# A second block product of layer two's token mixing taken as seven smaller ones, from sixteen more kept sums

## The chip, the cores and the metric

The kernel runs on one core of one Trainium2 chip. The metric is the time of one execution on the device, in microseconds (us); the median of several executions counts. The core has five engines with a queue of instructions each: PE (TensorE, matrix products into eight PSUM banks), DVE (VectorE), ACT (ScalarE), POOL (GpSimd) and SP (SyncE, which here only issues DMAs). Each works through its own queue in order and waits on semaphores for the others.

## The reference

One sequence of 2048 tokens with 512 features goes through a linear attention block, a gated MLP block, and both again, with the same weights ("layer one" and "layer two" are the two passes). The change lies in the second pass of this block:

```python
def _B_ref(x, w_in, w_sp, b_sp, w_out):          # x: 2048 x 512, normalised
    z = _gelu(jnp.einsum("bsd,df->bsf", x, w_in))          # 2 x 896 features
    z1 = z[..., :Fh]
    z2 = _layernorm(z[..., Fh:], axis=-1)
    g = jnp.einsum("ts,bsf->btf", w_sp, z2) + b_sp[None, :, None]   # w_sp: 2048 x 2048
    return jnp.einsum("bsf,fd->bsd", z1 * g, w_out)
```

The product with `w_sp` mixes tokens: every output token is a sum over all 2048 input tokens. All is float32.

## The kernel before

**Split operands.** Every float32 operand is taken as a rounded part h (type float32r, made by ACT) and a remainder l (made by DVE as source minus h). A product is three matmuls, h·h, h·l and l·h, added up in one PSUM bank.

**Stages of a layer.** `P1.run` goes over 16 tiles of 128 tokens and makes the attention's sums. `P2.run` goes over the tiles in steps s = 1 to 18, which I call token steps: attention output, layernorm, then `d_high`/`d_low` (the transposed input, split), `e` (the half of `w_in` that gives z2, matmuls of 448 columns), `f` (the half that gives z1, which is stored to DRAM), `e3`/`e4` (statistics and normalisation of z2). z2 stays in SBUF as `ztile[0]` to `ztile[15]`. `P4.run` then mixes tokens, and its last loop over 16 tiles multiplies by `w_out`.

**Mixing as seven products.** Output tokens and input tokens are halved. With 384 features on each side (`H1`, `H2`), the 2x2 block product is taken as seven products P1 to P7 of sums of blocks instead of eight. The 128 features left over (`H3`) go along in three of them (`WITH3`: P4, P1, P5). P3, P5, P6, P7 need sums of blocks of `w_sp`: POOL makes these in layer one (class `Sums`) and stores them to DRAM; both layers read them. P1, P2 and P4 read `w_sp` itself. `ORDERS` sets their order.

**Steps of the mixing.** `P4.run` has one loop over g. An ordinary product is 8 steps (128 input tokens each): 18 matmuls of 512 columns (two output blocks of 512 tokens, three feature tiles, three parts), 24 where `H3` goes along. In step g the kernel calls `prepare(g + 2, g + 3)` (split of the weights of step g+2 and of the tokens of step g+3), `mm(g)`, `fetch(g + 4)` (the DMA of later weights), then `gates()` and, at a product's end, `evac` (PSUM into the accumulators `unit(n, f)` in SBUF). `gates` handles at most one finished unit a step: it loads its z1 on SP, and one step later POOL multiplies (line 1389); a unit that P7 finishes needs a POOL subtraction before (line 1387, `both`).

**The nested product.** One product, P2 (output rows 1024 to 2047, input tokens 1024 to 2047, 512 columns `H1` and `H3`), is itself taken as seven, in 14 steps named "N" with 12 matmuls each (`NEST` gives their order). Three of the seven read `w_sp`; for the other four, sums of quarter blocks are made in layer one by class `Inner`: in 16 units (`todo`), each one DVE addition or subtraction of 128x512, one ACT high part, one DVE low part, two stores. They are read back already split, 1 MB a step, by a DMA that POOL issues (line 1177), so these steps have no weight split. On the token side, `token_sums` and `nested_low` make the sums of tokens, on DVE. Six "quad" buffers hold the weights, 22 "pages" of 128x512 nearly everything else; both are handed out in the order in which they were freed.

**Order around the change.** In layer one, `Inner`'s units stand in the token steps s = 13 to 18 and in the mixing; the nested product comes last, and no gate is handled in its steps 49 to 56. In layer two the order is P4, N, P1, P6, P7, P5, P3:

```python
ORDERS = ("P4", "P1", "P6", "P7", "P5", "P3", "P2"), ("P4", "P2", "P1", "P6", "P7", "P5", "P3")
```

Layer two's token steps also have products of their own (`self.seven`): `side`, `block_sums` and `block_parts`, from s = 14 on. All instructions stand in the order in which the Python code makes them; nothing is reordered by a scheduler.

Of the kernel before, what the change touches and what calls it, by code (L numbers as in the profile page):

```python
# [15 lines left out]
P = 128  # L16
# [40 lines left out]
def mixer_kernel(ctx: ExitStack, tc: tile.TileContext, x_in, wqkv, wo_d, win1_d, win2_d, wsp_d, bsp_d, wout_d,  # L57
# [550 lines left out]
    class P2:  # L608
# [309 lines left out]
        def run(self, sums):  # L918
            w1 = self.win1
            for s in range(1, NT + 3):  # L920
# [28 lines left out]
                else:  # L949
# [37 lines left out]
                if self.seven:  # L987
                    self.side(s)
                elif s == 12:
                    inner.begin(2)  # L990
                elif s == 13 or 15 <= s:
                    inner.unit()
# [61 lines left out]
    class Inner:  # L1054
# [3 lines left out]
        def __init__(self):  # L1058
            self.d = {m: dram.tile([2, P, 2, 2, 512], F32, name=f"n{m}") for m in range(1, 5)}
# [13 lines left out]
        def fetch(self):  # L1073

            if self.ahead:
                k, u = self.ahead.popleft()
                at = (((3, 8), (3, 12)), ((2, 8),), (), ((2, 12),))[u]
                for name, (n, s) in zip(("21", "22") if u == 0 else ("11",) if u == 1 else ("12",), at):
                    self.raw[name] = load(wsp_d[n, s + k])
# [58 lines left out]
    class P4:  # L1138
# [4 lines left out]
        ORDERS = ("P4", "P1", "P6", "P7", "P5", "P3", "P2"), ("P4", "P2", "P1", "P6", "P7", "P5", "P3")  # L1143
# [4 lines left out]
        OWN = {"P1": (2, 8), "P2": (2, 12), "P4": (3, 12)}  # L1148
        SUM = {"P3": 4, "P5": 1, "P6": 2, "P7": 3}

        def __init__(self, p2, sums):
# [5 lines left out]
            for p in self.ORDERS[p2.L]:  # L1157
                if p == "P2":
                    self.steps += [("N", d) for d in range(14)]
                else:  # L1160
                    self.steps += [(p, k) for k in range(HT)]
# [6 lines left out]
            self.wsteps = (48, 50, 51, 53, 55, 56, 57) if self.nest_late else range(54, 61)  # L1168
            self.wloads = (45, 47, 48, 50, 52, 53, 54) if self.nest_late else range(54, 61)

        def fetch(self, g):
# [3 lines left out]
            if p == "N" and self.NEST[k // 2] in self.SUM:  # L1175
                self.w[g] = quads.get([P, 2, 2, 512], F32R)
                nc.gpsimd.dma_start(self.w[g], inner.d[self.SUM[self.NEST[k // 2]]][k % 2])
                return
            t = quads.get([P, 2, 512])
            if p == "N":  # L1180
                n, s = self.OWN[self.NEST[k // 2]]
                s += 2 * (k % 2)
# [32 lines left out]
        def prepare(self, gw, gz):  # L1215
# [4 lines left out]
            if gw is not None:  # L1220
                r = self.raw.pop(gw)
                w = self.w[gw] = quads.get([P, 2, 2, 512], F32R)
                wh, wl = (w[:, :, i] if self.steps[gw][0] == "N" else w[:, i] for i in range(2))
                nc.scalar.activation(wh, r, AF.Copy)  # L1224
            inside = gz is not None and self.steps[gz][0] == "N"
# [25 lines left out]
        def token_sums(self, k):  # L1251
# [3 lines left out]
            a, b = ztile[8 + k], ztile[12 + k]  # L1255
# [3 lines left out]
        def nested_operand(self, g):  # L1259
            name, q = self.NEST[self.steps[g][1] // 2], self.steps[g][1] % 2  # L1260
# [4 lines left out]
            i, c = {"P1": (8, 0), "P2": (12, 0), "P3": (12, 256)}[name]  # L1265
            return name, q, [ztile[i + 2 * q + o][:, c:c + 256] for o in range(2)]
# [10 lines left out]
        def nested_low(self, g):  # L1277
# [7 lines left out]
            for o in range(2):  # L1285
                a, b = ztile[8 + 2 * q + o], ztile[12 + 2 * q + o]
# [7 lines left out]
        def nested_mm(self, g):  # L1294
            name, q = self.NEST[self.steps[g][1] // 2], self.steps[g][1] % 2
# [45 lines left out]
            if name == "P4" and self.nest_late:  # L1341
                self.ready.extend((n, f, False) for n in (2, 3) for f in range(4))

        def mm(self, g):
            p, k = self.steps[g]
            if p == "N":
# [4 lines left out]
            first, last = k == 0, k == HT - 1  # L1351
            if p in self.WITH3 and first:
                self.delta = [banks.get(PAGE) for _ in range(2)]
                self.beta = [[banks.get(PAGE) for _ in range(3)] for _ in range(2)]
# [3 lines left out]
            for j in range(2):  # L1358
                for f in range(3):
                    self.acc(self.beta[j][f], h, l, slice(f * P, (f + 1) * P), w, j,  # L1360
                             first and p in self.WITH3, last)
# [35 lines left out]
        def evac(self, p):  # L1397
# [3 lines left out]
            if p in ("P4", "P1", "P5"):  # L1401
                for j in range(2):
                    n = 2 + j if p == "P1" else j
                    held = p == "P5" or p == "P1" and not self.nest_late
# [4 lines left out]
            for j in range(2):  # L1409
                a, b = 2 + j, j  # L1410
                for f in range(3):
                    q = self.beta[j][f]
                    if p == "P1":
                        V.tensor_add(self.unit(a, f), bs[a] if self.nest_late else self.unit(a, f), q)
                        if not self.nest_late:
                            gates.append((a, f))
                    elif p == "P6":
                        V.tensor_add(self.unit(a, 4 + f), q, bs[a])
                    elif p == "P7":
                        V.tensor_sub(self.unit(b, 4 + f), bs[b], q)  # L1420
# [11 lines left out]
            self.ready.extend((n, f, p == "P7") for n, f in gates)  # L1432

# [53 lines left out]
        def run(self, nxt):  # L1487
# [14 lines left out]
            sums_at = self.steps.index(("N", 0)) - 3  # L1502
            for g in range(n):
# [8 lines left out]
                if self.nest_late:  # L1512
                    self.sums.tick(g, MIX_TICKS)
                    if g == MIX_UNITS[0] - 2:
                        inner.begin(2, 0)
                    if g + 2 in MIX_UNITS:
                        inner.fetch()
                    if g == 34:
                        inner.free = deque(range(8))
                    if g in MIX_UNITS:  # L1520
                        inner.unit(True)
                    elif MIX_UNITS[0] < g < 48:
                        inner.finish(True)
                if g == 3:
                    self.loadb()
                if sums_at <= g < sums_at + 4:
                    self.token_sums(g - sums_at)
# [14 lines left out]
                elif p != "N" and k == HT - 1:  # L1542
                    self.evac(p)
                if self.nest_late and g in (48, 60):
# [38 lines left out]
    inner = Inner()  # L1583
# [44 lines left out]
```

## Time and profile before

| | us |
|---|---|
| median of 3 runs | 1378.05 (1377.92 to 1378.29) |
| profiled execution | 1378.29 |
| its span, first to last instruction | 1376.6 |
| PE busy | 1370.5 |
| DVE busy | 962.5 |
| ACT busy | 606.2 |
| POOL busy | 447.5 |

Busy is time in which an instruction of the engine is under way. PE's matmuls overlap: each is shown with some 0.39 us, while they start about 0.23 us apart, so the starts tell PE's pace and the busy share cannot pass 100%. A DVE or POOL instruction that has begun and is held up counts as busy, too. In a timeline row the first number is the start, the second the length in us; brackets give the idle time of the engine before it and what ended that. A row of windows gives, for a stretch of the span, its length and each engine's busy time in it with the number of instructions.

### The profile page before, as it was taken

The page shows a single profiled execution, that of the slowest core. Times are in us where ns is not written, and L with a number is a line of the kernel's source. Part 1 is how long each engine was busy: PE and PEld are TensorE (multiplying, and loading weights), DVE is VectorE, ACT ScalarE, POOL GpSimd, SP SyncE. Part 2 cuts the span into 40 slices and gives each one's busy share as a digit, 9 for nine tenths or more (in the row PEclk, how much of TensorE's full clock was granted, in tenths as well). Part 3 has the DMA queues.
Part 4 walks back from the last instruction along what each step waited for, and adds up shares of the span by engine and source line. Part 5 has one row for each costly group of instructions (what it writes and reads, how often), then busy time and mean ns, then how long its engine had stood idle before and what let it go on. Part 6 is the DMA issues. An engine that isn't in the chain of part 4 may idle for free.

```text
span 1376.6 us, 17960 instructions
## 1 busy us (share of the span) xinstructions
PE 1370.5 (100%) x6185; PEld 1149.1 (83%) x6185; DVE 962.5 (70%) x1415; ACT 606.2 (44%) x954; POOL 447.5 (33%) x529
## 2 busy tenths in 40 slices
PE   9999999999999999999999999999999999999998
PEld 7888888888888888888888888888888888888887
DVE  6775888665756789887667858876667565775642
ACT  6675544444442442441357655443454342342410
POOL 3343375433233137424123425532220101133310
PEclk9999999999999999999999999999999999999999
DMA  5542377878778988887845414545365744444442
GB/s 173 173 131 62 115 243 254 246 255 279 252 258 285 312 272 275 269 332 249 294 130 152 137 48 143 182 161 164 116 204 178 290 128 135 166 135 155 168 146 91
DMA packets 161435, 267.07 MB, mean 194 GB/s; under 512 B 13760, under 2 KB 57664, under 8 KB 159296
## 3 DMA queue, kind: packets, MB, share of 16 engines
q1 hardware_dynamic: 155440, 242.73, 54.7%
q0 software_dynamic: 4032, 19.92, 4.0%
q10 hardware_dynamic: 1872, 3.28, 0.6%
q8 instruction: 48, 0.79, 0.2%
q14 instruction: 43, 0.35, 0.1%
HBM read 185.40 MB, written 80.48 MB: 193 GB/s over the span
## 4 chain that ended last, share of the span: by engine, by line
PE 99%; DVE 0%; DMA 0%; issue 0%; ACT 0%; DVEq 0%; ACTq 0%
PE bank L120 19%; PE bank L119 19%; PE bank L118 19%; PE bank L1369 11%; PE bank L1367 11%; PE bank L1368 11%; PE bank L1309 2%; PE bank L1311 2%; PE bank L1312 2%; PE bank L832 1%; PE bank L833 1%; PE bank L831 1%; PE bank L256 1%; PE bank L444 0%; DMA qd<-in_wsp_dram 0%; PE bank L475 0%
## 5 line engine op out<-in xcount | busy, mean ns | idle before, releaser
L1367 PE MATMUL bank<-qd,pg 128*128 128x512 f32 x672 | 261.4, 389 | 0.0
L1368 PE MATMUL bank<-qd,pg 128*128 128x512 f32 x672 | 261.4, 389 | 0.0
L1369 PE MATMUL bank<-qd,pg 128*128 128x512 f32 x672 | 261.4, 389 | 0.0
L1234 DVE TENSOR_TENSOR qd<-qd,qd 128x1024 fp32r<-128x1024 f32 x108 | 155.6, 1440 | 103.0 <-ACT qd L1224 101.3
L1224 ACT ACTIVATE qd<-qd 128x1024 fp32r<-128x1024 f32 x108 | 114.3, 1059 | 173.0 <-DMA qd<-s 68.0
L1389 POOL TENSOR_TENSOR bg<-bg,pg 128x512 f32<-128x512 f32 x56 | 83.8, 1504 | 203.3 <-DMA pg<-z 116.6
L120 PE MATMUL bank<-qd,pg 128*128 128x512 f32 x380 | 148.4, 390 | 0.0
L1368 PEld LDWEIGHTS bank<-qd,pg 128*128 128x128 f32 x672 | 126.1, 188 | 26.4
L1369 PEld LDWEIGHTS bank<-qd,pg 128*128 128x128 f32 x672 | 126.1, 188 | 26.1
L1367 PEld LDWEIGHTS bank<-qd,pg 128*128 128x128 f32 x672 | 126.1, 188 | 26.0
L233 POOL TENSOR_SCALAR rs<-mv 128x1 f32<-128x1 f32 x95 | 40.6, 427 | 317.6 <-DVE mv L231 316.1
L1033 POOL TENSOR_TENSOR pg<-pg,pg 128x512 f32<-128x512 f32 x64 | 93.6, 1462 | 138.9 <-DMA pg<-in_wsp_dram 79.6
L104 ACT ACTIVATE pg<-pg 128x512 fp32r<-128x512 f32 (+1 forms) x117 | 72.0, 618 | 130.6 <-DVE pg L295 45.4
L244 ACT ACTIVATE pg<-pg,nb,rs 128x512 f32<-128x512 f32 x63 | 51.1, 810 | 148.8 <-POOL nb L238 138.1
L118 PE MATMUL bank<-qd,pg 128*128 128x512 f32 x284 | 110.7, 390 | 0.0
L119 PE MATMUL bank<-qd,pg 128*128 128x512 f32 x284 | 110.6, 389 | 0.0
L107 DVE TENSOR_TENSOR pg<-pg,pg 128x512 fp32r<-128x512 f32 (+1 forms) x115 | 88.1, 768 | 18.1 <-ACT pg L104 11.2
L118 PE MATMUL bank<-bg,qd 128*128 128x448 f32 x256 | 94.0, 367 | 0.0
L119 PE MATMUL bank<-bg,qd 128*128 128x448 f32 x256 | 93.6, 366 | 0.0
L120 PE MATMUL bank<-bg,qd 128*128 128x448 f32 x256 | 93.4, 365 | 0.0
L295 DVE STREAM_TRANSPOSE pg<-pg 128x512 f32<-128x512 f32 x79 | 85.3, 1080 | 8.2 <-DMA x<-pg 2.3
L118 PE MATMUL bank<-wo,qd 128*128 128x512 f32 x224 | 87.1, 389 | 0.0
(192 smaller groups left out, 2953.4 us busy)
## 6 DMA issues: line engine op xcount, KB each, us to landing
qd<-s SPq DMA_DIRECT2D x64, 512.0 KB, 3.8
qd<-in_wsp_dram SPq DMA_DIRECT2D x44, 512.0 KB, 4.2
pg<-in_wsp_dram SPq DMA_DIRECT2D x80, 256.0 KB, 4.9
s<-pg SPq DMA_DIRECT2D x64, 256.0 KB, 4.4
qd<-n POOLq DMA_DIRECT2D x16, 1024.0 KB, 8.1
pg<-x SPq DMA_DIRECT2D x64, 256.0 KB, 3.5
pg<-z SPq DMA_DIRECT2D x56, 256.0 KB, 4.1
x<-pg SPq DMA_DIRECT2D x48, 256.0 KB, 3.0
```

The lines of the kernel that those rows point to most:

```text
L107: nc.vector.tensor_sub(l, src, h.bitcast(F32))
L118: nc.tensor.matmul(out, ah, bh, start=start, stop=False)
L119: nc.tensor.matmul(out, ah, bl, start=False, stop=False)
L120: nc.tensor.matmul(out, al, bh, start=False, stop=stop)
L295: nc.vector.transpose(y.rearrange("p c (t m) -> p m c t", m=4), r.rearrange("p (m c j) -> p m c j", m=4, c=4))
L1033: nc.gpsimd.tensor_tensor(t, a, b, op=OP.add)
L1224: nc.scalar.activation(wh, r, AF.Copy)
L1234: nc.vector.tensor_sub(wl, r, wh.bitcast(F32))
L1367: m(out, h[:, o], w[:, 0, j, :], start=start, stop=False, skip_group_check=True)
L1368: m(out, h[:, o], w[:, 1, j, :], start=False, stop=False, skip_group_check=True)
L1369: m(out, l[:, o], w[:, 0, j, :], start=False, stop=stop, skip_group_check=True)
L1389: nc.gpsimd.tensor_tensor(u, u, z1, op=OP.mult)
```

## The change

In layer two P1 (output rows 1024 to 2047, input tokens 0 to 1023, 512 columns) is taken as seven, too. There are now two `Inner` objects, `inner["N1"]` for P1 (base 0) and `inner["N2"]` for P2 (base 8), where base is the first of the eight tiles of input tokens. Layer one still computes P1 as before, and nests P2 alone.

- Layer two's order becomes P4, N1, P6, P7, N2, P5, P3: 68 steps instead of 62. N2, which stood second, now follows P7.
- The sixteen units of `inner["N1"]` are made in layer two's token steps 6 to 17: one a step between `d_high` and `d_low`, and one more after `side` in the steps 8, 10, 12, 14 and 16. The 17th call only finishes the 16th unit.
- P1's result no longer stays in PSUM for P6 to add to: N1 writes it to the units, P6 starts its banks anew, and `evac` of P6 adds the unit. `from_first`, called in the first six steps of P7, makes what P7 needs from it (eight DVE instructions of 128x512).

Lines in the order of the file (`onto` is true for N2 alone):

```diff
+            own = inner["N1" if self.seven else "N2"]
...
                         self.d_high(s - 2)
-                        if not self.seven and 14 <= s < 18:
-                            inner.unit()
+                        if 6 <= s < 18 if self.seven else 14 <= s < 18:
+                            own.unit()
                         self.d_low(s - 2)
...
                 if self.seven:
                     self.side(s)
+                    if s == 5:
+                        own.begin(4)
+                    elif s in (8, 10, 12, 14, 16):
+                        own.unit()
...
-        ORDERS = ("P4", "P1", "P6", "P7", "P5", "P3", "P2"), ("P4", "P2", "P1", "P6", "P7", "P5", "P3")
+        ORDERS = ("P4", "P1", "P6", "P7", "P5", "P3", "N2"), ("P4", "N1", "P6", "P7", "N2", "P5", "P3")
...
-                nc.gpsimd.dma_start(self.w[g], inner.d[self.SUM[self.NEST[k // 2]]][k % 2])
+                nc.gpsimd.dma_start(self.w[g], inner[p].d[self.SUM[self.NEST[k // 2]]][k % 2])
...
-                bs = {n: u[n] if self.nest_late else self.bs[2 + (n > 2)] for n in u}
+                bs = {n: u[n] if onto else self.bs[2 + (n > 2)] for n in u}
...
-            if name == "P4" and self.nest_late:
+            if name == "P4" and onto:
                 self.ready.extend((n, f, False) for n in (2, 3) for f in range(4))
...
+            start = first and (p in self.WITH3 or p == "P6" and self.L == 1)
...
                     elif p == "P6":
-                        V.tensor_add(self.unit(a, 4 + f), q, bs[a])
+                        V.tensor_add(self.unit(a, 4 + f), q, bs[a] if self.L == 0 else self.unit(a, f))
                     elif p == "P7":
-                        V.tensor_sub(self.unit(b, 4 + f), bs[b], q)
+                        V.tensor_sub(self.unit(b, 4 + f), bs[b] if self.L == 0 else self.unit(b, 4 + f), q)
                         gates.append((b, f))
...
+        def from_first(self, k):
+            V, (j, f) = nc.vector, divmod(k, 3)
+            if f == 0:
+                V.tensor_add(self.bs[j], self.bs[j], self.bs[2 + j])
+            V.tensor_sub(self.unit(j, 4 + f), self.bs[j], self.unit(2 + j, f))
...
-            sums_at = self.steps.index(("N", 0)) - 3
+            sums_at = [(m, self.steps.index((m, 0)) - 3) for m in ("N1", "N2") if (m, 0) in self.steps]
...
+                if not self.nest_late and p == "P7" and k < 6:
+                    self.from_first(k)
...
-    inner = Inner()
+    inner = {p: Inner(b) for p, b in (("N1", 0), ("N2", 8))}
```

More of the change, by code (lines that the diff above doesn't have):

```diff
@@ L1157, in __init__ @@
             for p in self.ORDERS[p2.L]:
[L1158 to L1161, printed above, removed]
+                self.steps += [(p, k) for k in range(14 if p[0] == "N" else HT)]
             self.T1, self.T2 = {}, {}
@@ L1222, in prepare @@
                 w = self.w[gw] = quads.get([P, 2, 2, 512], F32R)
-                wh, wl = (w[:, :, i] if self.steps[gw][0] == "N" else w[:, i] for i in range(2))
+                wh, wl = (w[:, :, i] if self.steps[gw][0][0] == "N" else w[:, i] for i in range(2))
                 nc.scalar.activation(wh, r, AF.Copy)
-            inside = gz is not None and self.steps[gz][0] == "N"
+            inside = gz is not None and self.steps[gz][0][0] == "N"
             if inside:
@@ L1360, in mm @@
                     self.acc(self.beta[j][f], h, l, slice(f * P, (f + 1) * P), w, j,
-                             first and p in self.WITH3, last)
+                             start, last)
             pages.put(h, l)
```

66 lines of the change are left out of this document (35 added, 31 removed).

## The prediction

> **What bounds the kernel now.** I read the page first: the engines' busy time, the chain that ended last, the costliest group.
>
> ```profile
> span 1376.6 us, 17960 instructions
> PE 1370.5 (100%) x6185; PEld 1149.1 (83%) x6185; DVE 962.5 (70%) x1415; ACT 606.2 (44%) x954; POOL 447.5 (33%) x529
> ...
> PE 99%; DVE 0%; DMA 0%; issue 0%; ACT 0%; DVEq 0%; ACTq 0%
> ...
> L1367 PE MATMUL bank<-qd,pg 128*128 128x512 f32 x672 | 261.4, 389 | 0.0
> ```
>
> The chain is PE for 99% of the span and PE idles nowhere that matters, so the time is the number of matmuls times PE's pace. The 389 ns of a matmul is not its price, because they overlap. Starts give the pace; these two timeline rows are the first matmuls of the nested product's first two steps, 12 matmuls apart:
>
> ```profile
> 1073.74 0.39 PE L1309 MATMUL bank<-qd,pg 128*128 128x512 f32 x1
> ...
> 1076.46 0.39 PE L1309 MATMUL bank<-qd,pg 128*128 128x512 f32 x1
> ```
>
> 2.72 us / 12 = 0.2267 us. Next I cut layer two's mixing at the starts of its products (windows, in this order: N, P1, P6, P7, P5):
>
> ```profile
> 1073.74:1111.83 38.09, 38.09 (x170) 31.55 (x169) 27.75 (x46) 15.70 (x26) 4.24 (x8) 1.00 0.82 299
> 1111.83:1155.34 43.51, 43.51 (x193) 36.05 (x192) 19.56 (x25) 12.86 (x18) 0.00 (x0) 1.00 0.32 101
> 1155.34:1187.98 32.64, 32.64 (x145) 27.04 (x144) 23.28 (x26) 11.37 (x15) 10.35 (x7) 1.00 0.58 194
> 1187.98:1220.62 32.64, 32.64 (x145) 27.04 (x144) 22.45 (x31) 13.40 (x20) 2.58 (x2) 1.00 0.40 129
> 1220.62:1264.14 43.52, 43.52 (x193) 36.05 (x192) 32.19 (x30) 14.09 (x21) 18.90 (x11) 1.00 0.40 133
> ```
>
> The columns are length, then PE, PEld, DVE, ACT, POOL, clock, DMA share, GB/s. N takes 168 x 0.2267 = 38.09 us and P1 192 x 0.2267 = 43.5: both run at PE's pace with the clock granted in full. POOL does nothing in N but issue eight DMAs, and DVE is busy for 73% of it. POOL is busy in P5: those are P7's gates.
>
> **The saving.** P1's 192 matmuls become N1's 168. 24 x 0.2267 = **5.44 us** less on the path. Nothing else on PE changes: P6 starts its banks with a flag instead of a matmul. All below asks what gives part of it back.
>
> **N1 and P6.** N1 stands where N stood, behind P4, with the same work on every engine and the same DMAs, so the first window is its cover: 0. P6 behind it needs less than P1 did: 0. `evac` of P6 is 6 DVE instructions as before. `from_first` adds eight DVE instructions of 128x512 to P7 and the four `token_sums` calls eight of 128x256, about 8 x 0.68 + 8 x 0.42 = 8.8 us by the last two of these groups (the first is ACT's high part, needed below):
>
> ```profile
> L104 ACT ACTIVATE pg<-pg 128x512 fp32r<-128x512 f32 (+1 forms) x117 | 72.0, 618 | 130.6 <-DVE pg L295 45.4
> ...
> L107 DVE TENSOR_TENSOR pg<-pg,pg 128x512 fp32r<-128x512 f32 x8 | 5.5, 684 | 0.0
> L1256 DVE TENSOR_TENSOR pg<-z_z 128x256 f32<-128x256 f32 x4 | 1.7, 419 | 0.0
> ```
>
> P7 then has 22.45 + 8.8 = 31.3 us of DVE work in 32.64, split weights are due two steps (8.2 us) later, and POOL is idle there once P1's gates are gone. Price 0; its cover is 1.3 us, and if that failed DVE would enter N2 late by as much.
>
> **The units in the token steps.** Each of the 16 adds one DVE sum and one DVE low part (2 x 0.68 = 1.37 us), one ACT part (0.62 us), one 256 KB load on average and two 256 KB stores on SP's queue. The stretches between successive `e` groups (from s = 6; s = 8; s = 16; s = 17; then two of layer one, where the same units already run):
>
> ```profile
> 867.33:880.38 13.05, 13.05 (x61) 11.27 (x60) 11.31 (x20) 5.66 (x10) 7.24 (x12) 1.00 0.69 214
> 893.44:906.49 13.05, 13.05 (x61) 11.27 (x60) 8.87 (x16) 4.94 (x8) 3.74 (x8) 1.00 0.50 161
> 985.62:993.24 7.62, 7.62 (x38) 6.76 (x36) 5.59 (x12) 4.45 (x7) 1.93 (x6) 1.00 0.32 107
> 993.24:1002.21 8.97, 8.97 (x43) 7.89 (x42) 7.48 (x15) 3.64 (x6) 3.09 (x8) 1.00 0.52 145
> 282.29:295.34 13.05, 13.05 (x62) 11.26 (x60) 8.52 (x15) 6.05 (x11) 3.19 (x6) 1.00 0.84 287
> 308.39:318.73 10.34, 10.34 (x50) 9.02 (x49) 7.36 (x14) 4.86 (x8) 3.91 (x8) 1.00 1.00 356
> ```
>
> With one or two units a stretch DVE has 11.31 + 0.7, 8.87 + 2.7, 5.59 + 2.7 and 7.48 + 0.7 us: over only at s = 16 (8.3 in 7.62), and s = 18 lies behind it. ACT has room everywhere (4.45 + 1.2 of 7.62 at s = 16). The tightest place is there, the transpose and low part that the `e` at 993.24 waits for:
>
> ```profile
> 987.44 1.07 DVE L295 STREAM_TRANSPOSE pg<-pg 128x512 f32<-128x512 f32 x1
> 990.33 0.69 DVE L107 TENSOR_TENSOR qd<-pg,qd 128x512 fp32r<-128x512 f32 x1 [1.82 <-ACT qd L104]
> ...
> 993.64 0.36 PE L120 MATMUL bank<-bg,qd 128*128 128x448 f32 x1
> ```
>
> The low part is ready at 991.02, 2.62 us before the first matmul that reads it. The unit stands between the two DVE rows, so its 1.37 us fall into the 1.82 us in which DVE waits for ACT. What the units of s = 14 and 15 leave over goes into the 2.62. DMA rises by 48 x 256 KB, about 90 GB/s over s = 6 to 17; layer one's stretches run at 287 and 356 GB/s with PE full. Price 0. Upper end: three units before that low part with nothing hidden, 4.1 - 2.62 = 1.5.
>
> **P7 into N2: what is late next.** P7's six gates used to fall into P5, steps of 5.44 us; now they fall into N2's steps of 2.72 us. SP is no obstacle, since N2's four middle products are fetched by POOL, so the z1 loads run ahead. But POOL's two instructions a gate meet DVE's splits. In P5 the timeline shows how they do (DVE rows, POOL rows, then POOL's two groups):
>
> ```profile
> 1217.42 4.09 DVE L1420 TENSOR_TENSOR bg<-pg,bank 128x512 f32<-128x512 f32 x6 [2.38 <-PE bank L1369]
> ...
> 1225.43 1.79 DVE L1240 TENSOR_TENSOR pg<-pg,pg 128x512 fp32r<-128x512 f32 x1
> 1227.14 1.64 DVE L1212 TENSOR_TENSOR pg<-z_z,z_z 128x384 f32<-128x384 f32 x1
> ...
> 1230.44 0.55 DVE L1212 TENSOR_TENSOR pg<-z_z,z_z 128x384 f32<-128x384 f32 x1
> ```
>
> ```profile
> 1218.19 1.29 POOL L1387 TENSOR_TENSOR bg<-bg 128x512 f32<-128x512 f32 x1 [28.52 <-DVE bg L1420]
> 1225.25 1.42 POOL L1389 TENSOR_TENSOR bg<-bg,pg 128x512 f32<-128x512 f32 x1 [5.76 <-DMA pg<-z]
> 1226.62 1.74 POOL L1387 TENSOR_TENSOR bg<-bg 128x512 f32<-128x512 f32 x1
> ```
>
> ```profile
> L1389 POOL TENSOR_TENSOR bg<-bg,pg 128x512 f32<-128x512 f32 x23 | 33.6, 1466 | 130.6 <-DVE qd L1234 68.8 <-DMA pg<-z 54.9 <-DVE bg L1428 4.3
> L1387 POOL TENSOR_TENSOR bg<-bg 128x512 f32<-128x512 f32 x6 | 12.1, 2023 | 28.5 <-DVE bg L1420 28.5
> ```
>
> They take turns. L1212 takes 0.55 us alone and 1.64 beside POOL; it ends 1.56 us after the L1240 before it (1227.22 to 1228.78), so POOL's turn cost DVE 1.56 - 0.55 = 1.01 us. The evacuation from PSUM at 1217.42 keeps 0.68 each with POOL at work.
>
> Let T be N2's start. Step d starts at T + 2.72 d and needs its low part 0.45 us later. POOL issues two DMAs first, the second when step 0 frees a buffer, 3.18 us in as in these rows of N, and 0.53 long; its first gate starts at T + 3.7:
>
> ```profile
> 1074.20 0.54 POOL L1177 DMA_DIRECT2D qd<-n  x1 [58.63 <-PE bank L1369]
> 1076.92 0.53 POOL L1177 DMA_DIRECT2D qd<-n  x1 [2.19 <-DVE qd L1234]
> ...
> DMA to landing us min/median/max: 5.0/7.1/8.4
> ```
>
> From there to the deadline of step 7 (T + 19.5) are 15.8 us. DVE has one weight split, four token splits and six half-width sums to do: 1.2 + 4 x 0.68 + 6 x 0.42 = 6.5 us. POOL's nine or ten turns take 9.1 to 10.1. Together 15.6 to 16.6: **0 to 0.8 us late**. Step 8 (18.5 us; DVE 8.0; POOL ten or eleven turns) comes to 18.1 to 19.1, the same. I take 0.8, because the quoted turns are strict. Lower end 0: POOL's DMA issues leave DVE free turns. Upper end: each turn costs POOL's full 1.30 us, 10 x 1.30 + 6.5 = 19.5, which is 3.7 late.
>
> POOL's own lateness is a second danger in the same place: its DMA for step 11 stands behind all six gates. With turns of 1.01 and some 0.5 us of DVE between, six gates and five DMA issues take 6 x 3.0 + 5 x 0.53 = 20.7 us: it is issued at T + 24.4 and lands 5.0 us later, at 29.4; step 11 starts at 29.9. At the groups' means (6 x 3.49 + 5 x 0.53 = 23.6) it lands 2.4 late, inside the upper end above, because PE held up at step 7 moves this deadline too. On SP the loads of N2's last two steps stand behind the six z1 loads; they are issued by step 8 or so and due at step 12: 0. N2 into P5 is N into P1 with one more 0.55 us sum a step. The single gates of N2 follow in P5, fewer than now: 0.
>
> **Sum.** -5.44 + 0.8 = -4.6 us. The profiled execution (1378.29, of it 1376.6 span) would go to 1373.7; it lies 0.24 above the median, so I forecast 1378.05 - 4.6 = **1373.4 us**. Ends: 1372.6 (nothing given back) and 1378.05 - 5.44 + 3.7 + 1.5 = 1377.8.
>
> **Rivals.**
> 1. *N2's turns cost POOL's whole instruction.* 3.7 us given back: 1376.3, of the size of no change. For it: strict turns, and twelve POOL instructions in six steps. Against: 1.01, not 1.30, in the rows above. The Trainium skill, SBUF — State Buffer, section "Who interferes with whom", says that a DVE instruction with two SBUF inputs and a GpSimd one that reads SBUF exclude each other for the whole instruction; by its rule the time is this rival's. The trace agrees on the exclusion and on PSUM inputs being free of it, and shows a shorter turn.
> 2. *Slower: units block DVE in the token steps.* A unit's sum waits at the head of DVE's queue for its load, and `d_low` stands behind it. Two units in a step leave some 6 us from load to use; loads of this kind take 4.5 us in layer one (row below), on an SP queue that also waits for ACT and DVE. Each step in which DVE is held for 0.65 us beyond the slack (2.6 to 5) costs that; over twelve steps 7.8 us, so 1381.2. It turns into a slowdown beyond 4.6 us. Against: layer one, full PE with the same units.
> 3. *The change doesn't do what it says.* 24 matmuls fewer is certain, so this has no share.
>
> ```profile
> pg<-in_wsp_dram SPq DMA_DIRECT2D x11, 256.0 KB, 4.5
> ```
>
> **How the numbers follow.** Forecast 0.66, with its own range 1372.4 to 1375.0; rival 1 0.22 (1375.0 to 1377.8); rival 2 0.12. A difference within 0.2% (2.76 us) is what a measurement of this kernel can hardly tell from none, so "faster" means below 1375.3: the forecast's share and some of rival 1, 0.70; same 0.18; slower 0.12. The range reaches from the forecast's lower end through most of rival 1: 1372.4 to 1377.2.
>
> **What would show it.** PE loses 24 matmuls and N1 takes 38.1 us. If I am right on N2, DVE's token splits there last 1.4 to 1.8 us, POOL is busy in its steps 1 to 8, and N2 takes 38.1 to 40.4 us with PE gaps only near steps 5 to 8 or 11. Rival 1 shows as N2 near 42 us; rival 2 as stretches between `e` groups longer than 13.05 and 10.33. I am wrong if PE idles in N1, P6, P7 or P5, or if the steps after N2 start late on weight splits.

## The result, and the profile after

The changed kernel takes 1384.49 us (median of 5 runs, 1383.84 to 1385.64) against 1378.05 for the kernel before (5 runs, 1377.92 to 1378.65): a ratio of 1.0047, 95% interval 1.0032 to 1.0062. It is slower by 6.4 us where 4.6 us less were forecast. The page of the changed kernel, its span, engines and chain:

```profile
span 1383.9 us, 18136 instructions
PE 1370.4 (99%) x6161; PEld 1145.6 (83%) x6161; DVE 998.5 (72%) x1487; ACT 617.0 (45%) x980; POOL 460.8 (33%) x537
...
PE 89%; DVE 5%; DMA 2%; ACT 2%; issue 1%; POOL 1%; SPq 0%; ACTq 0%; DVEq 0%; POOLq 0%
```

PE has its 24 matmuls less, but the chain, 99% PE before, now runs for a tenth of the span through other engines: somewhere PE waits. The windows of the changed kernel find the places: first the four stretches from the `e` of s = 14 to that of s = 18, then N1, P6, P7, N2, P5 (columns as in the prediction).

```profile
965.88:975.17 9.29, 9.14 (x43) 7.70 (x41) 6.65 (x12) 3.28 (x7) 2.87 (x6) 1.00 0.68 242
975.17:987.41 12.24, 10.83 (x48) 8.86 (x48) 8.52 (x15) 5.48 (x10) 3.43 (x6) 1.00 0.54 173
987.41:997.41 10.00, 8.15 (x36) 6.61 (x36) 8.23 (x17) 4.97 (x9) 2.90 (x6) 1.00 0.55 184
997.41:1008.42 11.01, 10.95 (x43) 9.21 (x43) 10.73 (x21) 6.62 (x11) 3.24 (x6) 0.85 0.76 234
1080.89:1118.97 38.08, 38.08 (x169) 31.53 (x168) 27.46 (x46) 15.37 (x26) 4.23 (x8) 1.00 0.83 303
1118.97:1151.61 32.64, 32.64 (x145) 27.03 (x144) 18.81 (x26) 11.91 (x17) 0.00 (x0) 1.00 0.41 130
1151.61:1184.25 32.64, 32.64 (x145) 27.03 (x144) 27.41 (x45) 13.56 (x21) 0.00 (x0) 1.00 0.41 138
1184.25:1227.73 43.48, 40.55 (x169) 32.49 (x168) 41.11 (x50) 13.72 (x24) 21.55 (x20) 0.96 0.84 294
1227.73:1271.25 43.52, 43.52 (x193) 36.04 (x192) 28.71 (x31) 15.17 (x23) 11.10 (x8) 1.00 0.44 146
```

The same four stretches took 8.97, 10.33, 7.62 and 8.97 us before (the last two rows stand in the prediction, the first two are these):

```profile
966.32:975.29 8.97, 8.97 (x43) 7.89 (x42) 5.57 (x9) 4.19 (x7) 2.12 (x6) 1.00 0.44 139
975.29:985.62 10.33, 10.33 (x49) 9.01 (x48) 7.59 (x15) 3.45 (x6) 1.25 (x4) 1.00 0.27 79
```

So 6.65 us are lost in the last token steps, a place that the prediction priced at 0. N2 takes 43.48 us instead of 38.09: 5.4 us lost, where 0.8 was expected. N1, P6, P7 and P5 are as forecast. With 0.9 us more at the start of the mixing (at 1040, where PE waits for DVE's late additions), -5.44 + 6.65 + 5.4 + 0.9 = +7.5 us; the span grew by 7.3. This profiled execution is the longest of the five (1385.64 us). In it PE's granted clock fell to half twice for 3.4 us, at 999.2 and 1207.4; the two executions with a mean granted clock of 1.000 took 1383.84 and 1383.90 us, so the slowdown does not rest on that.

**The token steps.** The first rows are from the timelines of the kernel before, tile 15 of the layernorm: the last of POOL's three small instructions (L233, L234, L238), then ACT's normalising (L244). The second group is the same tile after the change, on DVE, POOL, ACT and PE. (The line of an instruction can differ from kernel to kernel, since lines were added.)

```profile
988.66 0.27 POOL L238 TENSOR_SCALAR nb<-mv,rs 128x1 f32<-128x1 f32 x1
...
988.97 0.81 ACT L244 ACTIVATE pg<-pg,nb,rs 128x512 f32<-128x512 f32 x1 [1.37 <-POOL nb L238]
```

```profile
993.73 1.10 DVE L295 STREAM_TRANSPOSE pg<-pg 128x512 f32<-128x512 f32 x1
994.68 0.67 DVE L107 TENSOR_TENSOR pg<-pg,pg 128x512 fp32r<-128x512 f32 x1
995.27 0.66 DVE L1125 TENSOR_TENSOR pg<-pg,pg 128x512 f32<-128x512 f32 x1
997.39 0.69 DVE L107 TENSOR_TENSOR qd<-pg,qd 128x512 fp32r<-128x512 f32 x1 [1.46 <-ACT qd L104]
...
993.97 0.22 POOL L233 TENSOR_SCALAR rs<-mv 128x1 f32<-128x1 f32 x1 [0.93 <-ACT pg L839]
...
994.94 1.05 POOL L238 TENSOR_SCALAR nb<-mv,rs 128x1 f32<-128x1 f32 x1
...
996.03 0.81 ACT L244 ACTIVATE pg<-pg,nb,rs 128x512 f32<-128x512 f32 x1 [2.09 <-POOL nb L238]
996.75 0.61 ACT L104 ACTIVATE qd<-pg 128x512 fp32r<-128x512 f32 x1
...
995.22 0.39 PE L833 MATMUL bank<-qd,bg 128*128 128x512 f32 x1
997.41 0.47 PE L118 MATMUL bank<-bg,qd 128*128 128x448 f32 x1 [1.80 <-ACT qd L104]
```

The unit's low part and sum do start in DVE's gap behind the transpose. But POOL's `nb` is under way at that very time and takes 1.05 us instead of 0.27: it ends at 995.99, 0.06 us after the second of the two. ACT's normalising waits for `nb`, ACT's high part of the transposed input (of the tile before) queues behind it, DVE's low part and PE's `e` wait for that. So the gap does not fill: DVE still waits 1.46 us in it. From the end of DVE's aggregate (L231) to the end of `nb` it took 1.68 us for tiles 5 to 12 and 1.40 for 13 to 15 before; with a unit beside it, 2.74 and 2.17. Every step starts a little later on DVE, the lag adds up (layernorm's addition of tile 13 3.4 us later than before, of tile 15 6.3), and once it has used up the slack PE idles.

**N2.** DVE's, POOL's and PE's timelines around the longest gap, and the windows of that gap and behind it (L1395 and L1397 are a gate's subtraction and multiplication, L1387 and L1389 in the kernel before):

```profile
1200.46 1.77 DVE L107 TENSOR_TENSOR pg<-pg,pg 128x512 fp32r<-128x512 f32 x1
1202.27 3.00 DVE L1295 TENSOR_TENSOR pg<-z_z,z_z 128x256 f32<-128x256 f32 x2
...
1206.39 1.00 DVE L107 TENSOR_TENSOR pg<-pg,pg 128x512 fp32r<-128x512 f32 x1
...
1202.24 1.30 POOL L1395 TENSOR_TENSOR bg<-bg 128x512 f32<-128x512 f32 x1
1203.62 1.36 POOL L1397 TENSOR_TENSOR bg<-bg,pg 128x512 f32<-128x512 f32 x1
...
1204.96 0.39 PE L1317 MATMUL bank<-qd,pg 128*128 128x512 f32 x1
1207.44 0.79 PE L1318 MATMUL bank<-qd,pg 128*128 128x512 f32 x1 [2.09 <-DVE pg L107]
```

```profile
1204.96:1207.44 2.48, 0.39 (x3) 0.00 (x1) 2.45 (x5) 0.63 (x1) 2.38 (x4) 1.00 0.95 295
1207.44:1210.95 3.51, 3.51 (x8) 2.80 (x9) 3.51 (x6) 1.74 (x5) 1.61 (x2) 0.51 1.09 422
```

DVE is held by POOL's turns and its low part of step 7 comes at 1207.39, 23.1 us into N2 instead of 19.5. The gap before it is 2.48 us from start to start; the next eight matmuls then start 0.43 us apart at a granted clock of 0.51. In this execution that adds some 1.6 us to the waits.

### The profile page after: what moved, and what is told of

It reads as the page before. It is cut to its first block, busy times and chain, and to the rows that moved or that the text cites. A ratio compares the mean times of both kernels' runs of the same rounds, so it can differ in the third digit from the quotient of the medians.

```text
span 1383.9 us, 18136 instructions
## 1 busy us (share of the span) xinstructions
PE 1370.4 (99%) x6161; PEld 1145.6 (83%) x6161; DVE 998.5 (72%) x1487; ACT 617.0 (45%) x980; POOL 460.8 (33%) x537
## 4 chain that ended last, share of the span: by engine, by line
PE 89%; DVE 5%; DMA 2%; ACT 2%; issue 1%; POOL 1%; SPq 0%; ACTq 0%; DVEq 0%; POOLq 0%
PE bank L120 17%; PE bank L119 17%; PE bank L118 17%; PE bank L1375 10%; PE bank L1377 10%; PE bank L1376 10%; PE bank L1318 2%; PE bank L1315 2%; PE bank L1317 2%; DVE st L229 1%; DVE pg L107 1%; DMA qd<-in_wsp_dram 1%; PE bank L256 1%; DVE pg L1293 0%; POOL nb L238 0%
## 5 line engine op out<-in xcount | busy, mean ns | idle before, releaser
L1375 PE MATMUL bank<-qd,pg 128*128 128x512 f32 x608 | 236.8, 389 | 0.4 <-DVE pg L893 0.2
L1376 PE MATMUL bank<-qd,pg 128*128 128x512 f32 x608 | 236.6, 389 | 0.0
L1377 PE MATMUL bank<-qd,pg 128*128 128x512 f32 x608 | 236.6, 389 | 0.0
L1238 DVE TENSOR_TENSOR qd<-qd,qd 128x1024 fp32r<-128x1024 f32 x106 | 149.6, 1412 | 89.1 <-ACT qd L1228 88.6
L104 ACT ACTIVATE pg<-pg 128x512 fp32r<-128x512 f32 (+1 forms) x141 | 86.8, 619 | 163.4 <-DVE pg L295 48.3
L120 PE MATMUL bank<-qd,pg 128*128 128x512 f32 x380 | 148.4, 391 | 0.0
L233 POOL TENSOR_SCALAR rs<-mv 128x1 f32<-128x1 f32 x95 | 41.4, 436 | 315.0 <-DVE mv L231 313.5
L1375 PEld LDWEIGHTS bank<-qd,pg 128*128 128x128 f32 x608 | 114.1, 188 | 24.8 <-DVE pg L893 1.2
L1377 PEld LDWEIGHTS bank<-qd,pg 128*128 128x128 f32 x608 | 114.2, 188 | 23.7
L1376 PEld LDWEIGHTS bank<-qd,pg 128*128 128x128 f32 x608 | 114.2, 188 | 23.7
L1397 POOL TENSOR_TENSOR bg<-bg,pg 128x512 f32<-128x512 f32 x56 | 85.4, 1532 | 144.3 <-DMA pg<-z 123.5
L244 ACT ACTIVATE pg<-pg,nb,rs 128x512 f32<-128x512 f32 x63 | 51.0, 810 | 154.9 <-POOL nb L238 149.5
L118 PE MATMUL bank<-qd,pg 128*128 128x512 f32 x284 | 110.7, 390 | 0.0
L119 PE MATMUL bank<-qd,pg 128*128 128x512 f32 x284 | 110.6, 389 | 0.0
L107 DVE TENSOR_TENSOR pg<-pg,pg 128x512 fp32r<-128x512 f32 (+1 forms) x139 | 101.1, 729 | 10.0 <-DMA z<-pg 4.9
```

The costliest lines, as they stand in the source:

```text
L104: nc.scalar.activation(h, src, AF.Copy)
L107: nc.vector.tensor_sub(l, src, h.bitcast(F32))
L118: nc.tensor.matmul(out, ah, bh, start=start, stop=False)
L119: nc.tensor.matmul(out, ah, bl, start=False, stop=False)
L120: nc.tensor.matmul(out, al, bh, start=False, stop=stop)
L1238: nc.vector.tensor_sub(wl, r, wh.bitcast(F32))
```

## The experiments

Two losses, two questions: does each come from where the timelines point (units beside POOL's chain; turns beside DVE in N2), and is that all that stands between the seven products and their gain? Where an expectation gives a theory a letter, its own words say which theory is meant. "Lost" below is by how much PE's starts lie further apart than 0.227 us (512 columns) or 0.205 us (448), summed over a place. The kernel before ran beside each group on the same chip: 1377.82, 1377.82, 1377.80 and 1378.0 us.

**Without the units.** Layer two's calls of `own.unit()` go, and N1 multiplies N2's stored sums in place of its own.

```diff
-                        if 6 <= s < 18 if self.seven else 14 <= s < 18:
+                        if not self.seven and 14 <= s < 18:
                             own.unit()
...
-                    if s == 5:
-                        own.begin(4)
-                    elif s in (8, 10, 12, 14, 16):
-                        own.unit()
...
-                nc.gpsimd.dma_start(self.w[g], inner[p].d[self.SUM[self.NEST[k // 2]]][k % 2])
+                nc.gpsimd.dma_start(self.w[g], inner["N2"].d[self.SUM[self.NEST[k // 2]]][k % 2])
```

> The changed kernel without its sixteen units in layer two's token steps; N1 reads the kept sums that layer one made for the other block, so P1's values are wrong: what is left out is the making of N1's own sums. Theory (two separate losses: the units delay the token steps 14 to 17, and P7's gates delay N2): the four stretches between e groups that grew go back to 8.97, 10.33, 7.62 and 8.97 us, N2 still takes some 43 us; time 1384.5 - 6.7 - 0.9 (the late additions before the mixing) = about 1377. Rival (the units' DMAs or sums also cost later, or N2's loss is a consequence of the token steps): N2 is short too, about 1372.5. Rival (the loss in the token steps has another cause than the units): 1384.

1377.63 us, ratio 1.0000 [0.9991, 1.0009]. The four stretches are 8.97, 10.33, 7.61 and 8.97 us again, and N2 still loses 5.4. The units cost 6.9 us (1384.49 against 1377.63), and N2's loss does not come from the lag that they leave.

**The gates out of N2.** `gates` isn't called in g = 38 to 45, so the turns come later.

```diff
-                if not (self.nest_late and 49 <= g < 57):
+                if not (49 <= g < 57 if self.nest_late else 38 <= g < 46):
                     self.gates()
```

> The changed kernel with no gate handled in N2's steps 38 to 45, as layer one does it in its nested steps; the same work, eight steps later. Theory (POOL's turns against DVE make N2 late): N2 back to 38.1 us, token steps unchanged; 1384.5 - 5.3 = about 1379. Rival (N2 is late because of its weights or P7's evacuation): N2 stays at 43 us, 1384. Rival (the turns only move into P5): P5 grows by as much as N2 shrinks, 1384.

1388.33 us, ratio 1.0077 [1.0063, 1.0090]: worse. The profiled execution is the shortest of the five (1384.79); in it N2 takes 38.08 us, but P5 takes the loss, 6.1 us at its start:

```profile
1182.74:1220.82 38.08, 38.08 (x169) 31.54 (x168) 31.18 (x46) 11.01 (x19) 16.50 (x16) 1.00 0.92 338
1220.82:1270.43 49.61, 45.67 (x193) 36.97 (x192) 36.02 (x36) 17.87 (x27) 19.46 (x13) 0.97 0.37 132
```

The turns only moved, to the last 11 us of N2 and on into P5, where DVE splits the weights of P5's first steps (2.3 us each beside POOL, 1.2 alone) and evacuates N2's last sums behind them. What the longer executions lose in addition is open.

**Both edits.**

> Both edits together (N1's own sums left out as before). Theory: nothing gives the saving back, 1378.05 - 5.4 = 1372.6, at most 0.5 more. If the sum of the two is not met by more than 1 us, the two losses hang together.

1380.52 us, ratio 1.0020 [1.0012, 1.0029], 8 us above the expected 1372.6. The one loss left in layer two is 6.3 us at P5's start (in the profiled execution, 1378.73, the shortest): this run still holds the turns, only later, so it can't show whether the two losses add up. The run without units and with the gates in P5, below, does.

**All units early**, two a step in s = 6 to 13, none in the short last steps.

```diff
-                        if 6 <= s < 18 if self.seven else 14 <= s < 18:
+                        if 6 <= s < 15 if self.seven else 14 <= s < 18:
...
-                    elif s in (8, 10, 12, 14, 16):
+                    elif 6 <= s < 14:
```

> The changed kernel with its units two a step in steps 6 to 13, none in the short steps 15 to 17; same work. Theory A (the units fail because of the short steps, where DVE has no room): the token steps lose nothing, 1384.5 - 7.6 = about 1377. Theory B (each unit delays DVE's part for good and the delay adds up over the steps, so that where they stand hardly matters): the e groups of steps 10 to 14 are late instead, 1384 or more.

1387.08 us, ratio 1.0070 [1.0057, 1.0082]. The delay comes sooner: POOL's chain takes 2.74 us in six of these eight steps, DVE is 9.4 us late at tile 11, and the stretch of s = 12 takes 14.96 us instead of 13.05. Room in DVE's busy time (8.87 of 13.05 us at s = 8) is not what limits.

**Gates in P5.** None in g = 38 to 50, two a step in g = 51 to 59 (P5 is g = 52 to 59). All turns but one (at 1202.40) leave N2; the next is at 1224.82, 1.7 us into P5, when DVE has the splits for P5's first steps behind it.

```diff
-                if not (self.nest_late and 49 <= g < 57):
-                    self.gates()
+                if not (49 <= g < 57 if self.nest_late else 38 <= g < 51):
+                    self.gates(2 if not self.nest_late and 51 <= g < 60 else 1)
```

> The changed kernel with no gate handled in N2 from its first step on and two a step in the first P5 steps; same work. N2 had 27.8 us of DVE work in 38.1 us before, and twelve POOL turns of 1.01 us do not fit beside it; P5's stretch of 43.5 us has room for all fourteen gates (20 turns). Theory: N2 back to 38.1 us, P5 not longer than 44; the units' loss stays, so 1384.5 - 5.3 = about 1379. Rival (DVE is late in P5 instead, as when the gates were put eight steps later): P5 grows by 4 or more, 1383 to 1385.

1380.52 us, ratio 1.0020 [1.0011, 1.0030], 1.5 us above the expected 1379, but N2 and P5 run at PE's pace:

```profile
1185.08:1223.15 38.07, 38.07 (x169) 31.54 (x168) 30.67 (x50) 13.60 (x24) 5.53 (x9) 1.00 0.82 302
1223.15:1266.67 43.52, 43.52 (x193) 36.05 (x192) 42.77 (x31) 15.17 (x23) 34.66 (x19) 1.00 0.50 183
```

The first row also gives DVE's work in N2 with a single turn beside it: 30.67 us. In the changed kernel the same 50 instructions took 41.11, so the eleven further turns cost 10.4 us, 0.95 each, and 30.67 + 10.4 does not fit into 38.08. P5 bears the turns: DVE is busy there for 42.77 of 43.52 us and PE loses nothing.

**Half the turns.** The subtraction ahead of a gate (`both`) is left out in layer two, so that N2 has six POOL instructions instead of twelve.

```diff
-                if both:
+                if both and self.L == 0:
```

> The changed kernel without POOL's subtraction in P7's gates of layer two (left out: one of the two terms of those six units), so six POOL turns in N2 instead of twelve. Theory (turns): DVE's waits there fall from 12.2 us to 6, N2 loses at most 0.5 us, time about 1379.5. Rival (POOL's DMAs for the sums are issued too late): half the work before each issue helps them as well, but then the waits that end last in N2 are on those DMAs and not on DVE.

1383.48 us, ratio 1.0039 [1.0024, 1.0054]. N2 still loses 4.1 us, so the loss does not go with the number of turns; DVE is busy there for 37.80 us, so the five turns more than in the run before cost 7.1 us. DVE's and POOL's timelines:

```profile
1190.59 5.79 DVE L1293 TENSOR_TENSOR pg<-z_z,pg 128x256 f32<-128x256 f32 x2
1196.30 1.28 DVE L1330 TENSOR_TENSOR bg<-bank,bg 128x512 f32<-128x512 f32 x2
...
1190.87 1.30 POOL L1397 TENSOR_TENSOR bg<-bg,pg 128x512 f32<-128x512 f32 x1
1192.10 0.59 POOL L1181 DMA_DIRECT2D qd<-n  x1
1192.72 1.30 POOL L1397 TENSOR_TENSOR bg<-bg,pg 128x512 f32<-128x512 f32 x1
1193.95 0.59 POOL L1181 DMA_DIRECT2D qd<-n  x1
```

Two additions of 0.42 us take 5.79 (the first alone 4.39): it stays out over two of POOL's instructions and the DMA issues behind them, at which DVE gets no turn either. PE then idles: the start after 1194.49 comes 2.6 us later, at 1197.08, 0.1 us after the first of the two evacuations that stand behind the additions (L1330). The trace puts no wait of PE in N2 on a DMA of the sums, as the rival would have it.

**Units without DVE's two instructions** (the low part replaced by a second copy on ACT, the additions and subtractions left out).

```diff
-            low(l, t, h)
+            if self.base:
+                low(l, t, h)
+            else:
+                high(l, t)
...
-                nc.vector.tensor_add(t, self.raw["21"], t)
+                if self.base:
+                    nc.vector.tensor_add(t, self.raw["21"], t)
...
```

> The changed kernel whose units keep their loads, stores and buffers but have no DVE instruction: no sum is made, and the low part is a second copy by ACT (left out: N1's own sums). Theory (DVE's time, with or without POOL's small instructions behind it): the four late e groups of the token steps are on time again, 1384.5 - 7.5 = about 1377. Rival (the 12 MB of DMA or SP's longer queue make the transposed inputs late): they stay late, 1384.

1378.96 us, ratio 1.0009 [1.0000, 1.0018]. The stretches are 8.97, 10.33, 7.61 and 8.97 us and POOL's chain 1.68 and 1.40: loads, stores, SP's queue and ACT's parts are not the cause there. The time stays 1.3 us above the run without units; 0.65 of that shows in the trace at 1020, where PE waits for loads of `win_sums` that POOL issues.

**Units with one-input DVE instructions.** As above, with a statistics instruction (`bn_stats`) over the same 512 columns in place of each DVE instruction; nobody reads its result.

```diff
+        def look(self, t):
+            st = small.tile([P, 1, 6], F32, name="st", tag="st1")
+            nc.vector.bn_stats(st[:, 0, :], t)
...
-            low(l, t, h)
+            if self.base:
+                low(l, t, h)
+            else:
+                high(l, t)
+                self.look(h.bitcast(F32))
...
-                nc.vector.tensor_add(t, self.raw["21"], t)
+                if self.base:
+                    nc.vector.tensor_add(t, self.raw["21"], t)
+                else:
+                    self.look(t)
...
```

> The same, but with a statistics instruction of one SBUF input and the same length (0.69 us for 128x512) in the place of each DVE sum and low part. Theory A (DVE's time alone): the token steps lose as much as in the changed kernel, 6 to 7 us, about 1384. Theory B (the two-input instructions take turns with POOL's three small instructions between statistics and normalisation, which grew from about 1.4 to 2.2 us): the loss falls by 0.7 us a step and more, to 3 us or less, about 1380. Rival (DMA): as in the changed kernel, and also without DVE work.

1380.46 us, ratio 1.0017 [1.0008, 1.0027]. DVE spends the same time in the gap, but POOL is not held, and the low part follows after 0.72 us of waiting (DVE's and POOL's timelines, tile 15):

```profile
990.48 1.22 DVE L1074 BATCH_NORM_STATS2 st<-pg 128x6 f32<-128x512 f32 x2
992.42 0.69 DVE L107 TENSOR_TENSOR qd<-pg,qd 128x512 fp32r<-128x512 f32 x1 [0.72 <-ACT qd L104]
...
990.75 0.27 POOL L238 TENSOR_SCALAR nb<-mv,rs 128x1 f32<-128x1 f32 x1
```

The four stretches are as before. DVE's time as such fits the gap; what does not fit is two-input instructions beside POOL's chain. DVE's lag of 2.1 us at tile 15 remains and costs 2.0 us at 1017, where PE waits for loads of `win_sums`: POOL issues the first of them at 998.3, behind its small instructions, and at 996.2 in the kernel before.

**Units behind the layernorm.** The gates as in the fifth run, and a 128x1 copy of `nb` on DVE ahead of each unit, which makes DVE wait for the end of POOL's chain.

```diff
+            self.last_nb = self.ms[i][2]
...
                         if 6 <= s < 18 if self.seven else 14 <= s < 18:
+                            if self.seven:
+                                see = small.tile([P, 1], F32, name="see")
+                                nc.vector.tensor_copy(see, self.last_nb)
                             own.unit()
```

> With two turns a step of P5 in place of N2's, and in the token steps a 128x1 copy of the layernorm's last result (nb) on DVE ahead of each unit, so that DVE's unit instructions cannot start before POOL's chain has ended. Theory B (the unit's two-input instructions hurt only by holding POOL's layernorm chain): the chain stays at 1.68 and 1.40 us from aggregate to nb, the unit's 1.37 us fall beside ACT's normalising and high part (0.85 + 0.62 = 1.47 us), the four last token stretches come back to 8.97, 10.33, 7.61 and 8.97 us within 0.3 each, and the time is 5.4 us below before less what the later stretches keep: 1372.5 to 1375. Rival (it is DVE's added time in these steps, wherever it stands): the stretches stay as in the run with the turns in P5, and the time stays at 1380 to 1381.

1375.58 us, ratio 0.9984 [0.9975, 0.9992]: 2.2 us faster than the kernel before, 4.9 faster than the run with the gates in P5, 8.9 faster than the changed kernel. The interval excludes 1, so a difference below the 0.2% of the prediction can be told here. DVE's and POOL's timelines of tile 15, then the windows of the stretches of s = 16 and 17:

```profile
991.97 0.15 DVE L973 COPY see<-nb 128x1 f32<-128x1 f32 x1 [0.43 <-POOL nb L238]
992.04 0.68 DVE L107 TENSOR_TENSOR pg<-pg,pg 128x512 fp32r<-128x512 f32 x1
992.64 0.69 DVE L1129 TENSOR_TENSOR pg<-pg,pg 128x512 f32<-128x512 f32 x1
993.34 0.69 DVE L107 TENSOR_TENSOR qd<-pg,qd 128x512 fp32r<-128x512 f32 x1
...
991.67 0.27 POOL L238 TENSOR_SCALAR nb<-mv,rs 128x1 f32<-128x1 f32 x1
```

```profile
985.47:993.36 7.89, 7.78 (x37) 6.57 (x36) 7.28 (x17) 3.95 (x7) 2.12 (x6) 1.00 0.60 204
993.36:1002.85 9.49, 9.43 (x42) 7.92 (x43) 9.31 (x19) 6.79 (x11) 3.33 (x6) 1.00 0.71 231
```

An added wait of 0.43 us makes the step shorter: `nb` takes 0.27 us, the unit runs beside ACT's two instructions, and the low part follows without a gap. The stretches of s = 14 and 15 are back at 8.97 and 10.33 us, those of s = 16 and 17 at 7.89 and 9.49, the last 0.5 too long; so the time lies a little above the expected 1372.5 to 1375. A lag of 3.5 us against the run without units (below) is left at tile 15, and 1.5 us are lost around 1020, where PE waits for the loads of `win_sums`: POOL issues the first at 999.67, in the run without units at 995.74.

**Units behind the low part**, on the gates of the fifth run.

```diff
-                        if 6 <= s < 18 if self.seven else 14 <= s < 18:
+                        if not self.seven and 14 <= s < 18:
                             own.unit()
                         self.d_low(s - 2)
+                        if self.seven and 6 <= s < 18:
+                            own.unit()
```

> With two turns a step of P5 in place of N2's, and the token steps' unit behind DVE's low part of the tile in place of ahead of it. Theory B: POOL's chain of the same tile is over by then and stays at 1.68 and 1.40 us; the gap of 1.82 us ahead of the low part stays unused, and the unit's 1.37 us come on top of DVE's other work of the step. In the steps in which DVE has 1.4 us to spare nothing is lost; the last three stretches may grow by up to 1.4 us each: 1373 to 1378. Rival (added DVE time, wherever it stands): as the run with the turns in P5, 1380 to 1381.

1388.88 us, ratio 1.0081 [1.0067, 1.0095]: neither expectation. POOL's chain is 1.68 and 1.40 us as Theory B has it, and yet this is the slowest of all. The gap stays empty and a second one opens (DVE's and ACT's timelines):

```profile
931.33 0.56 DVE L752 TENSOR_TENSOR z_z<-z_z 128x384 f32<-128x384 f32 x1 [1.77 <-ACT z_z L244]
...
941.61 0.69 DVE L107 TENSOR_TENSOR qd<-pg,qd 128x512 fp32r<-128x512 f32 x1 [1.51 <-ACT qd L104]
...
942.82 0.68 DVE L1131 TENSOR_TENSOR pg<-pg,pg 128x512 f32<-128x512 f32 x1
...
943.54 0.63 ACT L104 ACTIVATE pg<-pg 128x512 fp32r<-128x512 f32 x1 [1.96 <-DVE pg L1131]
944.08 1.12 ACT L244 ACTIVATE z_z<-z_z,nb,rs 128x896 f32<-128x896 f32 x1
```

ACT's high part of the unit now comes late, z2's normalising queues behind it on ACT, and DVE's next step waits for that (the row at 931.33, of the step before: 1.77 us, where the run with the gates in P5 waits 0.85). Holding POOL's chain is the cause in the changed kernel, but not the only way to lose: a step is a loop through DVE, POOL, ACT and DVE again, and what is put on the loop can lengthen it.

**No units, gates in P5** (edits of the first and fifth runs; N1 reads N2's sums).

> With two turns a step of P5 in place of N2's, and no second set of sums made (N1 multiplies N2's sums, so the output's half is not the reference's): what the seven products are worth when neither loss is there. If the two losses are all that stood against the saved 5.44 us: 1372.4 to 1373.0. If a third stands behind them (N1's own loads or evacuations, P5's added turns): above 1374.

1372.97 us, ratio 0.9964 [0.9951, 0.9976], PE on 98% of the chain. The two losses were all that stood against the saving, up to 0.6 us (1377.80 - 5.44 = 1372.4). That the forecast 1373.4 lies near is luck: it has 0.8 us for turns in N2, of which this run has one.

**Second units in the long steps**, in s = 7, 8, 10, 11, 12 in place of 8, 10, 12, 14, 16, on the kernel with the copy of `nb`.

> The run with the units behind the layernorm, with the five second units of a step moved from the steps 8, 10, 12, 14 and 16 to 7, 8, 10, 11 and 12, so that none stands in the short last steps (10.33 and 7.61 us). Theory (what is left there, 0.7 us at 993, 1.54 at 1018 and 0.53 at 1036, is DVE's own lag, 3.5 us at tile 15, from too much work in the last short steps): the lag at tile 15 falls under 2 us, one to two microseconds come back: 1373.3 to 1374.7. Rival (the lag is bound to the number of units, and comes from the earlier steps as well): the lag is only moved ahead, and the time is that of the run before, 1375 to 1377.

1375.81 us, ratio 0.9985 [0.9976, 0.9994], no gain. DVE's lag against the run without units is 4.4 us at tile 12 (2.0 without this edit) and 4.6 at tile 15 (3.5): the rival held, the lag is only moved ahead. The 2.6 us between the run with the copy and the one without units are the price of the sixteen units, at their best place among those tried.

## Why the prediction missed

- **The saving, N1, P6 and P7, P5: right.** 24 matmuls less, N1 in 38.08 us, P6 and P7 in 32.64 each with `from_first` in P7, P5 in 43.52.
- **The units: wrong, and the largest error.** The step that failed is the one that lets the units' 1.37 us of a step fall into the gap in which DVE waits for ACT and prices them at 0. The gap was there because a chain ran through POOL, and the units' instructions lengthen that chain: 1.68 to 2.74 and 1.40 to 2.17 us. I had used the rule that a two-input DVE instruction and a POOL instruction exclude each other, but only for POOL's large gates; POOL's instructions of one column, a few tenths of a microsecond each, I overlooked. The Trainium skill, SBUF — State Buffer, section "Who interferes with whom", states the exclusion without a lower limit of size; the trace agrees (`nb` 0.27 to 1.05 us), and so do the run with one-input instructions and the one with the units behind `nb`.
- **Counting DVE's busy time per stretch was the wrong test.** "11.31 + 0.7" or "8.87 + 2.7" in 13.05 says nothing where DVE's step is a loop with waits in it. The second and third rows of the changed kernel's windows show it: DVE busy for 8.52 of 12.24 and 8.23 of 10.00 us, and PE late; so do the runs with the units early and behind the low part.
- **Rival 2's size was right and its mechanism wrong.** It priced the token steps at 7.8 us; 6.65 and 0.9 came, which is luck. Only the first unit waited for its load (0.86 us at 872.85, with PE on time): without DVE's two instructions the same loads and stores cost nothing in these steps and 1.3 us in all.
- **N2: mechanism right, size wrong.** POOL's turns, DVE's late low part of step 7 and a PE gap there are as described. The mis-sized term is DVE's 6.5 us up to step 7: it leaves out the four evacuations from PSUM that stand between (0.64 us each, 2.55 in all). From POOL's first gate to the end of step 7's low part DVE took 19.4 us where 15.8 were to be had. 8.7 of them are its own work, evacuations included, so POOL's eleven turns cost 0.97 us each on average, as I had it (1.01, with nine or ten); the low part came 3.6 us late, the size of rival 1 by luck, which had ten turns of 1.30 and no evacuations. The lower end assumed that POOL's DMA issues leave DVE free turns; the run with half the turns shows a DVE addition that got none at two of them. The whole of N2 would have shown it sooner: N's 27.75 us of DVE and twelve turns of 1.01 make 39.9, over 38.09. And the restart at half clock, 1.6 us in the profiled execution, was not foreseen.
- **The rivals were taken one at a time.** Two independent losses came together; their sum, 13 us, was no case of mine.

## What to carry to other kernels

Time in which an engine waits is free only if the new work does not slow what it waits for: follow the chain that ends the wait through every engine, down to its smallest instructions, and ask what the new instruction excludes. Here a wait added on purpose (DVE waits for POOL's last small result, then works beside ACT) turned a loss of 7.6 us (1380.52 against 1372.97) into one of 2.6. When turns of one engine are moved out of a stage, check the first deadlines of the stage that gets them: moved by eight steps, onto the splits for P5's first steps, they cost as much; moved behind those, two a step, they cost PE nothing in either stage.

## What the runs showed of the hardware

- Gaps of 2.1 to 2.6 us between PE's starts brought the granted clock down to 0.50 in about half the cases. Leaving out the first 20 us and what lies behind 1375, the fourteen traces have nineteen gaps of 2.10 to 2.62 us. Behind ten (2.19 to 2.60 us) the clock was 0.50 for 3.41 us, beginning 0 to 1.8 us after the restart, with 512 columns at 0.43 us and 448 at 0.37. Behind nine it stayed at 1.00, among them 2.49 us (all units early, at 1207.0) and 2.62 us (units behind the low part, at 1001.8). None of the eight gaps of 1.2 to 1.8 us brought it down. So the length alone does not decide; what else does, no run here shows. The Trainium skill, TensorE: Matmul & The Clock Gate, section "Why this matters for your kernels", warns of idle gaps over about 3 us; here ten shorter ones sufficed, and the measurement decides.
- In the run with half the turns a DVE addition of 0.42 us stayed out for 4.4 us while POOL went from a two-input instruction to a DMA issue and on to the next. With two POOL instructions ahead of each issue, as in the changed kernel, the longest that a single DVE instruction took there was 2.71 us (the 128x1024 one, 1.22 alone).
- Two DVE instructions in a row with two SBUF inputs (0.67 and 0.66 us) stretched a POOL instruction on 128x1 from 0.27 to 1.05 us: begun during the first, it ended 0.06 us after the second. One-input instructions of the same length left it at 0.27.
